# Two V groups between two score batches in a fused attention and gated MLP kernel

## The chip, the cores and the metric

One core of one Trainium2 chip. The metric is the device time of one execution in microseconds, the median of several runs. A profile of one execution gives the span from the first to the last instruction and the start of every instruction.

## The reference, cut to what matters

```python
x = A_x                                   # 1 x 2048 x 512, bf16
xn = layernorm(x)
# A: 32 heads of 16, causal window of 256 keys
qkv = xn @ wqkv                           # 512 x 1536
p = softmax(where(mask, q @ k.T * 16**-0.5, -1e9))
A = (p @ v) @ wo
# B: gate and up 512 x 1792, down 1792 x 512, no nonlinearity
B = ((xn @ w_gate) * (xn @ w_up)) @ w_down
return x + A + B
```

## The kernel before

Rows are taken in four chunks of 512. TensorE does four kinds of work. *Wide* matmuls (128 x 128 weights, 512 columns) do projections, gate, up, down and output. *Score batches* S (75 of them) use an array cut into 32 x 64 tiles and fill one PSUM tile of four banks, which one exp instruction of ScalarE empties into a P strip. *V groups* (16, one for each of the four groups `c` of eight heads in each chunk) use 64 x 32 tiles and add up two PSUM banks, which VectorE transposes. A generator issues the batches in order, and between them fills in wide work from one list, by a cost model in units of 0.216 us.

```python
self.ps_m = pool("ps_m", 4, space=PSUM)      # four banks for all wide work and V groups
self.ps_s = tc.tile_pool(name="ps_s", bufs=1, space=PSUM)   # one S tile, four banks
...
def values(self, T, c, accs=None):           # one V group
    accs = [self.ps_m.tile([128, 512], F32, tag="M", name="acc") for _ in range(2)]
    for i, (P, col, m, q, n) in enumerate(todo):          # 12 pieces (9 in chunk 0)
        for par in range(2):
            for e in range(4):
                nc.tensor.matmul(accs[par][32*e:32*e+32, q:q+n], lhsT=v, rhs=P[rows, e, col:col+n],
                                 tile_position=(64 * par, 32 * e), ...)
    for par in range(2):
        nc.vector.transpose(out=at[:, par]..., in_=accs[par][:])
...
# run(), cut: each V group follows a score batch, two batches after its own last one
for g, s in enumerate(steps):
    fill(-1, g)
    self.scores(*s)                          # S matmuls, exp, GpSimd masks
    upto = total * (g + 1) / len(steps)
    if values(g - LAG):                      # one V group, if one is due
        fill(min(spent + 4, upto), g)
        divide(g - LAG)                      # VectorE: reciprocal, multiply, transpose into OT
    for _, f in self.beside.get(g, ()):      # layernorm of the next chunk, a piece a batch
        f()
    fill(upto, g)                            # wide work
    self.mask_diag(*s)
```

The output of the chunk before, `down` and `wo`, is added to x by VectorE in `store` and leaves a `ps_m` bank there.

The softmax here doesn't subtract the row's maximum and nothing guards it: scores larger than these inputs give would overflow.

## Time and profile before

| | before |
|---|---|
| time | 266.61 us (median of 3, 266.38 to 267.07) |
| span of the profiled run | 264.5 us |
| TensorE busy | 98%, clock 1.0 |
| VectorE, ScalarE, GpSimd busy | 67%, 66%, 43% |

A busy TensorE is not the same as a streaming one. Its matmuls overlap in the records (a wide one is 0.38 us long there, and in a row one starts every 0.216 us), so what counts is the distance from one start to the next. The prediction below shows the lines and works on those distances.

### The profile page before, as it was taken

How to read it: one execution, taken by the hardware profiler on the slowest of the kernel's cores; microseconds unless marked ns; L12 is line 12 of the kernel's file. 1: busy time of each engine (PE TensorE's matmuls, PEld its weight loads, DVE VectorE, ACT ScalarE, POOL GpSimd, SP SyncE). 2: the span in 40 equal slices, each digit the busy share in tenths (PEclk: the TensorE clock that was granted, in tenths of full speed). 3: DMA queues.
4: the chain of work that ended last, by engine and by line, in shares of the span. 5: the costliest groups of instructions: out<-in, count | busy, mean ns of one | idle time of the engine just before them, and what ended most of it. 6: DMA issues, size and time to landing. Idle time of an engine off the chain costs nothing.

```text
span 264.5 us, 8898 instructions
## 1 busy us (share of the span) xinstructions
PE 258.2 (98%) x3869; PEld 120.1 (45%) x3890; DVE 178.2 (67%) x344; ACT 174.5 (66%) x139; POOL 114.9 (43%) x278
## 2 busy tenths in 40 slices
PE   8999999999999999999999999999999999999995
PEld 8444444444444444444444444444444444444453
DVE  6677898787757667667765866766752576867244
ACT  3467687788556678687765667668766576867500
POOL 6125333326674535334575443534354353344600
PEclk9999999999999999999999999999999999999999
DMA  6999911120131000002022100000200010000002
GB/s 190 379 351 342 276 21 22 24 47 4 20 90 34 22 2 1 2 2 47 2 59 66 40 2 2 0 2 4 48 2 20 25 41 2 2 0 2 4 2 79
DMA packets 19431, 15.12 MB, mean 57 GB/s; under 512 B 7360, under 2 KB 19392, under 8 KB 19392
## 3 DMA queue, kind: packets, MB, share of 16 engines
q1 hardware_dynamic: 18848, 14.26, 18.4%
q8 instruction: 30, 0.49, 0.8%
q10 hardware_dynamic: 544, 0.30, 0.4%
q14 instruction: 9, 0.07, 0.1%
HBM read 9.70 MB, written 2.10 MB: 45 GB/s over the span
## 4 chain that ended last, share of the span: by engine, by line
PE 98%; issue 1%; DVE 0%
PE up L400 19%; PE gp L389 19%; PE psd L420 16%; PE qkp L248 11%; PE S L304 10%; PE acc L358 7%; PE vp L236 5%; PE psd L426 5%; PE L L420 2%; PE wps L122 2%; PE L L426 1%; PE L L358 0%; PE xTp L207 0%; DVE y L435 0%; DVE idle L89 0%
## 5 line engine op out<-in xcount | busy, mean ns | idle before, releaser
L311 ACT ACTIVATE P<-S 128x2048 bf16<-128x2048 f32 x75 | 140.7, 1876 | 47.4 <-PE S L304 39.9
L156 POOL TENSOR_SCALAR_AFFINE_SELECT P<-P 64x256 bf16<-64x256 bf16 x224 | 98.8, 441 | 128.5 <-ACT P L311 117.6
L400 PE MATMUL up<-xnT,Wu 128*128 128x512 bf16 x224 | 60.0, 380 | 0.0
L389 PE MATMUL gp<-xnT,Wg 128*128 128x512 bf16 x224 | 58.9, 380 | 0.0
L404 DVE TENSOR_TENSOR hT<-up,gsb 128x512 bf16<-128x512 f32 x56 | 38.5, 687 | 19.5 <-PE up L400 18.0
L420 PE MATMUL psd<-Wd,hT 128*128 128x512 bf16 (+1 forms) x195 | 46.8, 368 | 1.9 <-issue 1.7
L335 DVE TENSOR_TENSOR P<-P,diag 128x512 bf16<-128x512 bf16 (+1 forms) x75 | 29.7, 397 | 10.0 <-ACT P L311 10.0
L420 PEld LDWEIGHTS <-hT 128*128 128x128 bf16 x238 | 21.2, 98 | 25.0 <-issue 2.7
L389 PEld LDWEIGHTS <-Wg 128*128 128x128 bf16 x224 | 20.7, 98 | 25.6 <-issue 1.9
L364 DVE STREAM_TRANSPOSE at<-acc 128x512 f32<-128x512 f32 x30 | 19.7, 696 | 18.6 <-PE acc L358 18.6
L400 PEld LDWEIGHTS <-Wu 128*128 128x128 bf16 x224 | 19.9, 98 | 25.0 <-issue 3.3
L304 PE MATMUL S<-Q,K 16*64 16x320 bf16 (+4 forms) x720 | 31.0, 260 | 0.1
L304 PE MATMUL S<-Q,Ko 32*64 32x320 bf16 (+4 forms) x720 | 30.9, 260 | 0.0
L227 ACT ACTIVATE gsb<-gp 128x512 bf16<-128x512 f32 x34 | 20.0, 596 | 15.5 <-PE gp L389 13.5
L248 PE MATMUL qkp<-xnT,Wqkv 128*128 128x512 bf16 x128 | 30.0, 380 | 0.0
L304 PEld LDWEIGHTS <-K 16*64 16x64 bf16 x720 | 12.1, 103 | 31.8 <-issue 31.4
L358 PE MATMUL acc<-P,VS 64*32 64x320 bf16 (+4 forms) x672 | 18.7, 254 | 0.0
L358 PE MATMUL acc<-P,V 64*32 64x320 bf16 (+4 forms) x672 | 18.5, 254 | 0.0
L248 PEld LDWEIGHTS <-Wqkv 128*128 128x128 bf16 x128 | 11.7, 98 | 14.6 <-issue 1.6
L229 DVE CAST gsb<-gp 128x512 bf16<-128x512 f32 x22 | 15.2, 691 | 3.4 <-PE gp L389 2.0
L426 PE MATMUL psd<-Wo,OT 128*128 128x512 bf16 (+1 forms) x59 | 16.2, 369 | 0.2 <-issue 0.2
L358 PEld LDWEIGHTS <-V 64*32 64x32 bf16 x720 | 14.5, 90 | 3.2 <-issue 2.6
(54 smaller groups left out, 197.0 us busy)
## 6 DMA issues: line engine op xcount, KB each, us to landing
out_dram<-y SPq DMA_DIRECT2D x15, 128.0 KB, 1.7
Wg<-in_B_w_gate_dram SPq DMA_DIRECT2D x2, 896.0 KB, 11.3
Wu<-in_B_w_up_dram SPq DMA_DIRECT2D x2, 896.0 KB, 12.5
Wd<-in_B_w_down_dram SPq DMA_DIRECT2D x1, 1792.0 KB, 17.0
Wqkv<-in_A_wqkv_dram SPq DMA_DIRECT2D x3, 512.0 KB, 6.2
x<-in_A_x_dram SPq DMA_DIRECT2D x2, 512.0 KB, 8.1
VS<-V SPq DMA_DIRECT2D x6, 144.0 KB, 2.6
x<-in_A_x_dram SPq DMA_DIRECT2D x3, 256.0 KB, 6.7
```

Of the source, the lines that this page charges most:

```text
L156: nc.gpsimd.affine_select(out=v, in_=v, pattern=pattern + [[1 if diag else -1, 64]], compare_op=ALU.is_ge if diag else ALU.is_gt, fill=0.0 ...
L227: nc.scalar.activation(out=out, in_=in_, func=ACT.Copy)
L248: nc.tensor.matmul(ps[:], lhsT=self.Wqkv[:, k, lo:lo + 128], rhs=self.xnT[T][:, :, k, :], start=(k == 0), stop=(k == 3))
L304: nc.tensor.matmul(S[64 * par:64 * par + 64, e, col:col + n], lhsT=(self.Ko if par else self.K)[U][rows, c, keys], rhs=self.Q[T][rows, c, ...
L311: nc.scalar.activation(out=P[:, :, 0:col], in_=S[:, :, 0:col], func=ACT.Exp, scale=0.25)
L335: self.nc.vector.tensor_tensor(out=v, in0=v, op=ALU.min, in1=self.diag.unsqueeze(1).unsqueeze(1).to_broadcast([128, 4, n, 64]))
L358: nc.tensor.matmul(accs[par][32 * e:32 * e + 32, q:q + n], lhsT=v, rhs=P[rows, e, col:col + n], start=(i == 0), stop=(i == len(todo) - 1), ...
L389: nc.tensor.matmul(ps[:], lhsT=self.Wg[:, k, 128 * f:128 * f + 128], rhs=self.xnT[T][:, :, k, :], start=(k == 0), stop=(k == 3))
L400: nc.tensor.matmul(ps[:], lhsT=self.Wu[:, k, 128 * f:128 * f + 128], rhs=self.xnT[T][:, :, k, :], start=(k == 0), stop=(k == 3))
L404: nc.vector.tensor_tensor(out=self.hT[T][:, f, :], in0=ps[:], in1=self.gsb[:], op=ALU.mult)
L420: nc.tensor.matmul(ps, lhsT=self.hT[T][:, f, 128 * b:128 * b + 128], rhs=self.Wd[:, f, c0:c1], start=(f == 0), stop=False)
L426: self.nc.tensor.matmul(ps, lhsT=self.OT[T][:, c, 128 * b:128 * b + 128], rhs=self.Wo[:, c, c0:c1], start=False, stop=(c == 3))
```

## The change

The intent: when two V groups stand together, with a score batch on both sides, TensorE changes its array shape four times for what took six. The places are shifted so that blocks of TensorE's instructions (in the trace of the kernel before, 30 packets of 16 KiB on an instruction queue, q8 of its DMA view) arrive in time, and score batches keep a minimum distance so that none waits for the exp before it. The diff, cut to its core:

```diff
+SCORES, VALUES, SECOND = 1.9, 6.0, 5.0
+FIRST = 3
+GAP = 9.6
+PAIRS = ((0,), (1,), (2,), (3,)), ((0, 1), (2, 3)), ((0, 1), (2, 3)), ((0, 1), (2,))
+SHIFT = {20: -2, 21: -5, 22: -8, 23: -11, 24: -14, 26: -10, 27: -7, 28: -3, 62: 3, 63: 6, 64: 8, 66: 8, 67: 6, 68: 4, 69: 2}
+MASKED, FIRST_DIVIDE, SECOND_DIVIDE = 8, 8, 24
-        self.ppool = pool("ppool", 7)
-        self.xpool = pool("xpool", 4)
-        self.ypool = pool("ypool", 4)
+        self.qpool, kpool, hpool ...            # Q, K, Ko and hT in tiles of one slice
+        self.ppool = pool("ppool", 11)
-            self.OT[T] = self.chunk2.tile(...)  # two buffers
+            self.OT[T] = self.work1.tile(...)   # one buffer
-        y = self.ypool.tile(...); add(out=y, in0=ps, in1=self.x[:, t, c0:c1])
+        y = self.x[:, t, c0:c1];  add(out=y, in0=ps, in1=y)
-    self.beside[self.first[T, 0] + (0, 2, 3, 4, 5)[i]] = fs      # layernorm of the next chunk
+    self.beside[self.first[T, 0] + (5, 6, 7, 8, 9)[i]] = fs
+    gu(T, range(FIRST))                         # three gate and up slices ahead of the downs
...
+    upto = max(total * (g + 1) / len(steps) + SHIFT.get(g, 0), spent + GAP)
+    for i, key in enumerate(keys):
+        self.values(*key)                       # one or two V groups
+    if len(keys) == 2:
+        held = s, keys                          # the next batch follows at once;
+        continue                                # masks and divides come later
```

More of the change, by code (lines that the diff above doesn't have):

```diff
@@ L23 @@
 REST = (((0, *SIX), (1, *SIX), (0, *FOUR)), ((1, *FOUR), (2, *FOUR)), ((2, *SIX), (3, *SIX), (3, *FOUR)))
-SCORES, VALUES = 1.9, 6.0
+SCORES, VALUES, SECOND = 1.9, 6.0, 5.0
[4 more added lines that the diff above has]
+MASKED, FIRST_DIVIDE, SECOND_DIVIDE = 8, 8, 24
 COPY = dict(act=2.8, dve=3.2)
@@ L43, in __init__ @@
         self.chunk2 = pool("chunk2", 2)
-        self.chunk3 = pool("chunk3", 3)
-        self.ppool = pool("ppool", 7)
+        self.qpool = pool("qpool", 5)
+        self.kpool = pool("kpool", 9)
+        self.hpool = pool("hpool", self.NF + FIRST)
+        self.ppool = pool("ppool", 11)
         self.work = pool("work", 2)
-        self.xpool = pool("xpool", 4)
         self.small = pool("small", 4)
-        self.ypool = pool("ypool", 4)
         self.work1 = pool("work1", 1)
@@ L111, in setup @@
             self.triangle(self.far[half], False)
-        self.xnT, self.Q, self.hT, self.O, self.OT = {}, {}, {}, {}, {}
+        self.xnT, self.Q, self.hT, self.OT = {}, {}, {}, {}
         self.K, self.Ko, self.V, self.VS = {}, {}, {}, {}
@@ L124, in new_chunk @@
     def new_chunk(self, T):
-        self.Q[T] = self.chunk2.tile([128, 4, 512], BF16, tag="Q", name=f"Q{T}")
-        self.K[T] = self.chunk3.tile([128, 4, 512], BF16, tag="K", name=f"K{T}")
-        self.Ko[T] = self.chunk3.tile([128, 4, 512], BF16, tag="Ko", name=f"Ko{T}")
         self.V[T], self.VS[T] = self.stock[T % 3]
@@ L186, in norm_apply @@
         mv, j, rs = self.stats.pop(t)
-        xn = self.xpool.tile([128, 512], BF16, tag="xn", name="xn")
+        xn = self.work.tile([128, 512], BF16, tag="xn", name="xn")
         nc.vector.tensor_scalar(out=xn[:], in0=self.x[:, t, :], scalar1=mv[:, j, 0:1],
@@ L210, in bank @@
     def bank(self, ks, name):
+        self.open = 3 not in ks
         if 0 in ks:
@@ L251, in proj_qk @@
             return
-        self.copy((self.K if is_k else self.Q)[T][:, c, :], ps[:], engine)
         if is_k:
-            nc.vector.tensor_scalar(out=self.Ko[T][:, c, :], in0=self.K[T][:, c, :],
+            self.K[T, c] = self.kpool.tile([128, 512], BF16, tag="K", name="K")
+            self.Ko[T, c] = self.kpool.tile([128, 512], BF16, tag="Ko", name="Ko")
+        else:
+            self.Q[T, c] = self.qpool.tile([128, 512], BF16, tag="Q", name="Q")
+        self.copy((self.K if is_k else self.Q)[T, c][:], ps[:], engine)
+        if is_k:
+            nc.vector.tensor_scalar(out=self.Ko[T, c][:], in0=self.K[T, c][:],
                                     scalar1=self.odd[:, 0:1], scalar2=None, op0=ALU.mult)
@@ L304, in scores @@
                     nc.tensor.matmul(S[64 * par:64 * par + 64, e, col:col + n],
-                                     lhsT=(self.Ko if par else self.K)[U][rows, c, keys],
-                                     rhs=self.Q[T][rows, c, q:q + n],
+                                     lhsT=(self.Ko if par else self.K)[U, c][rows, keys],
+                                     rhs=self.Q[T, c][rows, q:q + n],
                                      start=True, stop=True, tile_position=(32 * e, 64 * par),
@@ L360, in values @@
                                      tile_position=(64 * par, 32 * e), skip_group_check=True)
-        at = self.work1.tile([128, 2, 16, 32], F32, tag="at", name="at")
+        at = self.work.tile([128, 2, 16, 32], F32, tag="at", name="at")
         for par in range(2):
@@ L374, in divide @@
         if c == 0:
-            self.OT[T] = self.chunk2.tile([128, 4, 512], BF16, tag="OT", name=f"OT{T}")
-        on = self.work.tile([128, 16, 2, 16], BF16, tag="on", name="on")
+            self.OT[T] = self.work1.tile([128, 4, 512], BF16, tag="OT", name=f"OT{T}")
+        on = self.work1.tile([128, 16, 2, 16], BF16, tag="on", name="on")
         nc.vector.tensor_tensor(out=on.rearrange("p b r d -> p r b d"), in0=at[:, :, :, 0:16],
@@ L384, in gate @@
         nc = self.nc
-        if f == 0 and 0 in ks:
-            self.hT[T] = self.const.tile([128, self.NF, 512], BF16, tag="hT", name=f"hT{T}")
         ps = self.bank(ks, "gp")
@@ L403, in up @@
             return
-        nc.vector.tensor_tensor(out=self.hT[T][:, f, :], in0=ps[:], in1=self.gsb[:], op=ALU.mult)
+        self.hT[T, f] = self.hpool.tile([128, 512], BF16, tag="hT", name="hT")
+        nc.vector.tensor_tensor(out=self.hT[T, f][:], in0=ps[:], in1=self.gsb[:], op=ALU.mult)
         self.book("dve", COPY["dve"])
@@ L409, in down @@
         nc = self.nc
+        self.open = True
         if lo == 0 and part == 0:
@@ L419, in down @@
             ps, c0, c1 = self.sums[b][part]
-            nc.tensor.matmul(ps, lhsT=self.hT[T][:, f, 128 * b:128 * b + 128],
+            nc.tensor.matmul(ps, lhsT=self.hT[T, f][:, 128 * b:128 * b + 128],
                              rhs=self.Wd[:, f, c0:c1], start=(f == 0), stop=False)
@@ L431, in store @@
         nc = self.nc
+        self.open = False
         t = 4 * T + b
         ps, c0, c1 = self.sums[b][part]
-        y = self.ypool.tile([128, 512], BF16, tag="y", name="y")[:, 0:c1 - c0]
-        nc.vector.tensor_tensor(out=y, in0=ps, in1=self.x[:, t, c0:c1], op=ALU.add)
+        y = self.x[:, t, c0:c1]
+        nc.vector.tensor_tensor(out=y, in0=ps, in1=y, op=ALU.add)
         self.book("dve", COPY["dve"])
@@ L463, in project, with gu @@
                 qk(T, c, self.first[T, c])
-        def gu(T, between):
-            for f in range(NF):
+        def gu(T, fs, between={}):
+            for f in fs:
                 for ks in halves:
@@ L498, in fillers @@
                     for i, fs in norms(T + 1, 0, 1).items():
-                        self.beside[self.first[T, 0] + (0, 2, 3, 4, 5)[i]] = fs
-                down(T - 1, 0)
-                wo(T - 1, 0, (0, 1))
+                        self.beside[self.first[T, 0] + (5, 6, 7, 8, 9)[i]] = fs
+                gu(T, range(FIRST))
                 for b in range(4):
-                    if b < 3:
-                        down(T - 1, b + 1, range(0, NF - 2, 2))
-                    wo(T - 1, b, (2, 3))
+                    down(T - 1, b)
+                    wo(T - 1, b, range(4))
                     add(0, lambda T=T, b=b: self.store(T - 1, b))
-                    if b < 3:
-                        down(T - 1, b + 1, range(NF - 2, NF, 2))
-                        wo(T - 1, b + 1, (0, 1))
-            gu(T, norms(1, 1, 3) if T == 0 else {})
+                gu(T, range(FIRST, NF))
+            else:
+                gu(T, range(NF), norms(1, 1, 3))
             if T + 1 < NCH:
@@ L523, in run @@
         self.setup()
-        NCH, LAG = self.NCH, 2
+        NCH = self.NCH
         RESERVE = 31.5
@@ L533, in run @@
                 steps.append((T, pieces))
-        due = {g: key for key, g in self.last.items()}
+        due = {}
+        for T in range(NCH):
+            for cs in PAIRS[T]:
+                due[self.last[T, cs[-1]] + 3 - len(cs)] = [(T, c) for c in cs]
         self.beside = {}
         work = self.fillers()
-        total = sum(w[0] for w in work) - RESERVE + SCORES * len(steps) + VALUES * (len(due) - 1)
+        total = sum(w[0] for w in work) - RESERVE + SCORES * len(steps)
+        total += sum(VALUES + SECOND * (len(keys) - 1) for keys in due.values())
         spent, n = 0, 0
         self.free = dict(act=0, dve=0)
-        valued, ready = -1, -1
+        valued, ready, pending = -1, -1, []
         def fill(upto, group):
@@ L554, in fill, with divide @@
                 n += 1
-        def values(g):
-            nonlocal spent
-            if g not in due:
-                return False
-            spent += VALUES
-            self.now = spent
-            self.values(*due[g])
-            return True
-        def divide(g):
+                while pending and spent >= pending[0][0]:
+                    pending.pop(0)[1]()
+        def divide(key):
             nonlocal ready
-            self.divide(*due[g])
-            ready = g
+            self.divide(*key)
+            ready = self.last[key]
+        held = None
         for g, s in enumerate(steps):
-            fill(-1, g)
-            valued = ready
+            keys = due.get(g, [])
+            if held is None:
+                valued = ready
+                fill(-1, g + len(keys) // 2)
+                while len(keys) == 2 and self.open:
+                    fill(spent + work[n][0] / 2, g)
             spent += SCORES
@@ L575, in run @@
             self.scores(*s)
-            upto = total * (g + 1) / len(steps)
+            upto = max(total * (g + 1) / len(steps) + SHIFT.get(g, 0), spent + GAP)
             if g in (1, 2):
                 self.new_values()
-            if values(g - LAG):
+            for i, key in enumerate(keys):
+                spent += SECOND if i else VALUES
+                self.now = spent
+                self.values(*key)
+            if len(keys) == 2:
+                held = s, keys
+                continue
+            if held is not None:
+                pending += [(spent + MASKED, lambda s=held[0]: self.mask_diag(*s)),
+                            (spent + FIRST_DIVIDE, lambda key=held[1][0]: divide(key)),
+                            (spent + SECOND_DIVIDE, lambda key=held[1][1]: divide(key))]
+                held = None
+            for key in keys:
                 fill(min(spent + 4, upto), g)
-                divide(g - LAG)
+                divide(key)
             for _, f in self.beside.get(g, ()):
@@ L593, in run @@
         fill(spent + 10, -1)
-        self.values(*due[len(steps) - 1], self.late)
+        self.values(T, 3, self.late)
         spent += VALUES
-        divide(len(steps) - 1)
+        divide((T, 3))
         valued = ready
```

## The prediction

> **What bounds the kernel now.** I read the page's busy table first, then the chain that ended last, the waits of TensorE, and last the timeline of one trip of TensorE from wide matmuls through a score batch and a V group and back.
>
> ```profile
> PE 258.2 (98%) x3869; PEld 120.1 (45%) x3890; DVE 178.2 (67%) x344; ACT 174.5 (66%) x139; POOL 114.9 (43%) x278
> PE   8999999999999999999999999999999999999995
> PEclk9999999999999999999999999999999999999999
> PE 98%; issue 1%; DVE 0%
> ```
>
> TensorE (PE) is busy in every slice at the full granted clock, VectorE and ScalarE are a third idle, and the chain that sets the end is 98% TensorE. Only less work or fewer bubbles on TensorE can shorten the program. Does TensorE wait for anybody? The waits view of that engine has four rows in all:
>
> ```profile
> PE psd L420 <- issue: 1.7, 11, 0.2
> PE wps L122 <- DVE idle L89: 1.1, 1, 1.1
> PE psd L426 <- issue: 0.2, 1, 0.2
> PE L L420 <- issue: 0.2, 1, 0.2
> ```
>
> The 1.1 us is the start. The others are 13 gaps of 0.2 us, each the length of one wide matmul. The busy table has 3869 matmuls beside 3890 weight loads, so 21 records are missing, and I read these gaps as missing records, not as idle time. So no wait for another engine is there to be removed. What remains is time that is busy on paper but streams nothing, and only start-to-start distances show it. The timeline of TensorE, lines left out inside the V group:
>
> ```profile
> 110.14 1.03 PE L400 MATMUL up<-xnT,Wu 128*128 128x512 bf16 x4
> 111.10 0.28 PE L304 MATMUL S<-Q,K 16*64 16x192 bf16 x4
> 111.11 0.28 PE L304 MATMUL S<-Q,Ko 32*64 32x192 bf16 x4
> 111.20 0.30 PE L304 MATMUL S<-Q,K 16*64 16x320 bf16 x4
> 111.22 0.30 PE L304 MATMUL S<-Q,Ko 32*64 32x320 bf16 x4
> 111.45 0.26 PE L358 MATMUL acc<-P,V 64*32 64x192 bf16 x4
> ...
> 112.50 0.29 PE L358 MATMUL acc<-P,VS 64*32 64x256 bf16 x4
> 112.73 0.60 PE L389 MATMUL gp<-xnT,Wg 128*128 128x512 bf16 x2
> ```
>
> Inside a row of wide matmuls one starts every 0.216 us (four of them, 0.38 us long each, span 1.03). The last of the four starts at 110.79 and the score batch at 111.10: 0.309 us, so 0.093 us more than streaming. The last score matmul starts at about 111.23 and streams 320 columns, 0.133 us at 2.4 columns per ns; V starts at 111.45, 0.224 later: 0.091 lost. V's last matmul, 256 columns (0.107 us), starts at about 112.53; the wide ones resume 0.202 us later: 0.095 lost. Over all 75 score batches and 16 V groups the medians of these distances are the same: wide to S 0.309, S to V 0.224, V to wide 0.202, S to wide 0.227 (0.094 lost). After a return the first two wide matmuls are 0.227 apart and not 0.216: another 0.011. So **each change of array shape costs about 0.093 us** wherever it occurs. The 75 batches and 16 groups make 167 changes, some 15.5 us of the 264.5.
>
> [...]its instruction queue of TensorE moves 0.49 MB in 30 packets, 16 KiB each, and in the packet records they take 0.91 to 1.92 us, median 1.08. [...]No run yet shows a stall from it: the twelve V groups of the later chunks, 192 instructions each, all have 1.077 to 1.080 us between first and last start.
>
> **The change part by part.** Before, each V group follows a score batch of its own: wide, S, V, wide, three changes of shape. After, for chunks 1 and 2 (two pairs each) and chunk 3 (one pair), two V groups stand between two score batches: wide, S, V, V, S, wide. Chunk 0 and the last two heads groups of chunk 3 stay single. Five pairs.
>
> Two trips before: 2 x (0.093 + 0.091 + 0.095 + 0.011) = 0.580 us of loss.
> One double trip after: wide to S 0.093, S to V 0.091, V to V about 0.010, V to S about 0.094, S to wide 0.094, first pair of wide ones 0.011: 0.393 us.
> V to V keeps the shape. A V group has 12 pieces; 1.079 us to its last start, less 0.96 us for the 2304 columns before the last piece, leaves 0.12 for 11 boundaries, so 0.010 each. V to S doesn't occur before; I take the price of the other changes.
> **Saving: 0.187 us a pair, 0.93 us for five.** All of it is on the path, since TensorE waits for nobody and is the chain.
>
> The rest of the diff moves no TensorE time by itself. The count of matmuls is the same. Q, K, Ko and hT become tiles of one slice each, P gets 11 buffers in place of 7, the result is written over x in place of a y buffer: these allow the new order (the first head group's five strips live longer: five and five batches and the one just issued make 11) and add no instruction. Three gate and up slices now come before the down projections of the chunk before, and norm work moves by a few batches; same work. The new minimum distance between score batches (9.6 units of 0.216 us, 2.07 us of wide work) prevents a wait that the kernel before doesn't have: all 75 batches start 0.309 us after the last wide matmul (the longer ones by a missing record), and the closest pair of batches is 2.71 us apart.
>
> 266.61 - 0.93 = 265.68, say **265.7 us**.
>
> **The rivals.**
> *Instruction fetch takes it back.* A pair issues 2 x (32 to 48) + 2 x 192, so 448 to 480 instructions, in about 3.2 us (0.36 + 1.19 + 1.28 + 0.36). 256 instructions then last 1.6 us in the V groups, against 1.08 us for the transfer of a block[...]; today a block lasts 3.5 us at the least (shortest interval between packets). Against it: the change picks its five places for this, by shifts of single batches. For it: the margin is under 0.5 us, and it was set by trial. If half the pairs lose 0.5 us, the time is about 267; if all five lose 1 us, 270.
> *The second score batch waits for exp.* There is one S buffer. From S to the second S there are 0.35 + 1.19 + 1.28 = 2.82 us. An exp starts 0.56 us after its batch's first matmul (median of 75) and takes 1.88, done at 2.44; today's closest batch comes 0.24 us after the exp's end without delay. Slack 0.14 to 0.38 us. A PSUM copy of 0.60 us just ahead of the exp would turn it into 0.1 to 0.3 us of waiting: at worst 1.5 us over five pairs, 267.
> *PSUM banks.* Two V groups hold all four buffers of the shared pool. The transposes of a group are done 0.72 and 1.32 us after its last matmul. The first group's are done within V's second 1.19 us and the score batch; the second group's are needed only after two more banks of wide work, 0.36 + 1.73 us later. Slack of about 0.8 us, unless VectorE has other work in front; the masks and divides are deferred for that. Likely nothing, at worst 0.5 us.
> *More is gained than the switches.* There is no wait to remove, so I see no way below about 265.
>
> **Range and chances.** The middle is 265.7. The repeats of the kernel before spread by 0.7 us (266.38 to 267.07), so the median of three is good to some 0.3. One or two pairs with a stall of half a microsecond give 266.2 to 266.7. I take 265.1 to 266.6 for 8 in 10. Faster by over 2% would need 261.3, six times the saving: 1%. Slower by over 2% needs 271.9, a stall of over 1 us in each pair: 2%. Within 2%: 97%.
>
> **What would show each step.** Right: five places in the timeline with S, V, V, S; 157 changes of shape in place of 167; [...]V to S losing some 0.09; a shorter span with the same matmuls; and still no wait of TensorE for ScalarE, VectorE or anything else. Wrong: V starts inside a pair further apart than 0.01 us beyond streaming (fetch), a wait of S for exp or of wide matmuls for the transposes, or a last stretch, after the last V group, that is longer than the 11.5 us of before because the pacing leaves too little wide work there.

The rate of 2.4 columns per ns is in the trace of the kernel before (512 columns every 0.216 us). The 256 instructions of a block are near what the same trace gives as a mean, 257: from the start of the first packet to that of the thirtieth 3732 weight loads start, each with its matmul, so 7464 instructions over 29 packets. The chances and sizes of the stalls (half a microsecond, one microsecond) were estimates.

## The result

| | before | changed |
|---|---|---|
| time, 6 runs each | 266.39 us (266.23 to 267.07) | 265.39 us (265.04 to 265.44) |
| span of the profiled run | 264.5 us | 263.7 us |
| first score batch to start of last V group (trace) | 239.48 us | 238.70 us |

The ratio is 0.9956 (95% interval 0.9943 to 0.9969). Ratios here are the mean time of one kernel's runs over that of the other's of the same rounds, so not quite the ratio of the medians. The result is 1.0 us faster, within 2%, inside the predicted range and near the predicted 265.7.

The third row of the table is the measure that I use from here on: from the first matmul of the first score batch to the first matmul of the last V group. Both kernels do the same TensorE work in that stretch (3650 weight loads, each with its matmul), and it leaves out the start, which varies by some tenths of a microsecond between profiles, and the end.

The changed kernel's page, its busy table, TensorE's row of slices and the chain that ended last:

```profile
PE 259.6 (98%) x3890; PEld 120.3 (46%) x3890; DVE 174.2 (66%) x341; ACT 175.9 (67%) x142; POOL 117.3 (44%) x278
PE   7999999999999999999999999999999999999995
PE 97%; DVE 1%; DMA 1%; issue 0%
```

This time all 3890 matmuls are recorded, and the 13 gaps called "issue" of the kernel before are gone, so they were missing records indeed. TensorE is the bound as before. Its waits:

```profile
PE wps L127 <- DVE idle L94: 1.1, 1, 1.1
PE xTp L209 <- DVE xn L190: 0.3, 1, 0.3
```

Both are at the start. By this view nobody holds TensorE up later. The timeline of TensorE at pair 2 (wide, S, V, V, S, wide; the lines inside the V groups left out) shows the new trip:

```profile
123.31 0.81 PE L251 MATMUL qkp<-xnT,Wqkv 128*128 128x512 bf16 x3
124.05 0.28 PE L312 MATMUL S<-Q,K 16*64 16x192 bf16 x4
...
124.41 0.26 PE L366 MATMUL acc<-P,V 64*32 64x192 bf16 x4
...
125.46 0.29 PE L366 MATMUL acc<-P,VS 64*32 64x256 bf16 x4
125.54 0.27 PE L366 MATMUL acc<-P,V 64*32 64x192 bf16 x4
...
126.58 0.29 PE L366 MATMUL acc<-P,VS 64*32 64x256 bf16 x4
126.81 0.28 PE L312 MATMUL S<-Q,K 16*64 16x192 bf16 x4
...
126.93 0.30 PE L312 MATMUL S<-Q,Ko 32*64 32x320 bf16 x4
127.16 1.04 PE L251 MATMUL qkp<-xnT,Wqkv 128*128 128x512 bf16 x4
```

The first V group's last matmul starts at 125.49 (the fourth of the row at 125.46) and the second group begins 0.051 us later, although that last matmul, of 256 columns, streams for 0.107. (The rate is in the traces: V to wide takes 0.149 us after a last piece of 128 columns and 0.202 after one of 256, so 2.4 columns per ns.) At a change of shape the same distance is 0.199 to 0.202. So V to V doesn't just avoid the price of a change of shape, it overlaps, by 0.056 us.

**Counting one pair cleanly.** Before, two trips take, in distances from start to start, 2 x (0.130 within S + 0.224 + 1.079 within V + 0.202) plus 2 x (0.093 + 0.011) at the wide work: 3.478 us. Pair 2 takes 0.130 + 0.224 + 2.200 + 0.199 + 0.130 + 0.226, plus 0.104: 3.213 us. The saving is **0.265 us a pair**, 1.325 us for five. The trace shows only 239.48 - 238.70 = 0.78 us. Where is the other half microsecond? The five pairs don't look alike. Their V runs, from the first to the last start, in the first profile:

| pair | 1 | 2 | 3 | 4 | 5 |
|---|---|---|---|---|---|
| V run, ns | 2357 | 2200 | 2401 | 2199 | 2369 |

Pairs 1, 3 and 5 lose 0.157, 0.201 and 0.169 us, together 0.53, and 1.325 - 0.53 = 0.80. That closes the account. The waits view doesn't show these losses: the recorded end of a matmul lies after its streaming (0.29 us after the start at 256 columns, which stream for 0.107), so a short wait disappears under it.

**Pair 1.** The timeline of all engines there:

```profile
89.25 0.57 POOL L182 TENSOR_TENSOR rs<-ve,mhalf 128x1 f32<-128x1 f32 x1
...
89.85 0.48 DVE L190 TENSOR_SCALAR xn<-x,mv,rs 128x512 bf16<-128x512 bf16 x1 [1.27 <-POOL rs L182]
...
90.25 0.67 DVE L444 TENSOR_TENSOR x<-psd,x 128x512 bf16<-128x512 f32 x1
...
90.76 0.29 PE L366 MATMUL acc<-P,VS 64*32 64x256 bf16 x4
...
90.98 0.26 PE L366 MATMUL acc<-P,V 64*32 64x192 bf16 x4
```

The second V group's first piece starts 0.256 us after the piece before it, and not 0.109 as in pair 2. Its weight load waits on VectorE's semaphore alone and starts 0.06 us after VectorE has finished (90.92) the output add that empties a bank. (The matmul itself waits on GpSimd's semaphore; GpSimd's masks had ended at 90.67.) That add stood in VectorE's queue behind a layernorm instruction, xn, which had waited 1.27 us for GpSimd's rs. Pair 3 has the same pattern: its second V matmul row starts at 155.73, just after a VectorE copy that ended at 155.67 and had itself come after an xn that waited 1.27 us for rs.

**Pair 5.** TensorE's timeline:

```profile
222.71 0.27 PE L366 MATMUL acc<-P,V 64*32 64x192 bf16 x4
222.76 0.49 PE L366 MATMUL acc<-P,VS 64*32 64x320 bf16 x4
222.95 0.32 PE L366 MATMUL acc<-P,V 64*32 64x320 bf16 x4
```

Here a gap of 0.165 us from start to start lies in the middle of a group, before a matmul that waits on no semaphore. The trace's record of the last block packet before it in TensorE's instruction queue has it from 220.59 to 221.55.

### The profile page after: what moved, and what is told of

Same layout as the page of the kernel before. It is cut to its first block, busy times and chain, and to the rows that moved or that the text cites. A ratio compares the mean times of both kernels' runs of the same rounds, so it can differ in the third digit from the quotient of the medians.

```text
span 263.7 us, 8896 instructions
## 1 busy us (share of the span) xinstructions
PE 259.6 (98%) x3890; PEld 120.3 (46%) x3890; DVE 174.2 (66%) x341; ACT 175.9 (67%) x142; POOL 117.3 (44%) x278
## 4 chain that ended last, share of the span: by engine, by line
PE 97%; DVE 1%; DMA 1%; issue 0%
PE gp L395 19%; PE up L406 19%; PE psd L428 17%; PE qkp L251 11%; PE S L312 10%; PE acc L366 7%; PE vp L239 5%; PE psd L434 5%; PE L L428 2%; DMA x<-in_A_x_dram 1%; DVE st L169 1%; PE L L434 1%; PE L L366 0%; PE xTp L209 0%; DVE xn L190 0%; DVE mv L170 0%
## 5 line engine op out<-in xcount | busy, mean ns | idle before, releaser
L158 POOL TENSOR_SCALAR_AFFINE_SELECT P<-P 64x256 bf16<-64x256 bf16 x224 | 101.3, 452 | 126.0 <-ACT P L319 111.6
L395 PE MATMUL gp<-xnT,Wg 128*128 128x512 bf16 x224 | 60.2, 380 | 0.0
L406 PE MATMUL up<-xnT,Wu 128*128 128x512 bf16 x224 | 58.8, 380 | 0.0
L428 PE MATMUL psd<-Wd,hT 128*128 128x512 bf16 (+1 forms) x210 | 48.0, 369 | 0.0
L343 DVE TENSOR_TENSOR P<-P,diag 128x512 bf16<-128x512 bf16 (+1 forms) x75 | 29.1, 388 | 9.5 <-ACT P L319 9.5
L406 PEld LDWEIGHTS <-Wu 128*128 128x128 bf16 x224 | 20.6, 98 | 25.6 <-issue 2.3
L230 ACT ACTIVATE gsb<-gp 128x512 bf16<-128x512 f32 x40 | 23.5, 596 | 7.5 <-PE gp L395 6.7
L444 DVE TENSOR_TENSOR x<-psd,x 128x512 bf16<-128x512 f32 (+1 forms) x15 | 9.7, 653 | 16.4 <-PE psd L434 16.4
L251 PEld LDWEIGHTS <-Wqkv 128*128 128x128 bf16 x128 | 11.7, 98 | 14.5 <-issue 1.6
L366 PE MATMUL acc<-P,VS 64*32 64x320 bf16 (+4 forms) x672 | 18.0, 253 | 0.0
L239 PE MATMUL vp<-Wqkv,xnT 128*128 128x512 bf16 x64 | 15.3, 380 | 0.0
```

The lines of the kernel that those rows point to most:

```text
L158: nc.gpsimd.affine_select(out=v, in_=v, pattern=pattern + [[1 if diag else -1, 64]], compare_op=ALU.is_ge if diag else ALU.is_gt, fill=0.0 ...
L230: nc.scalar.activation(out=out, in_=in_, func=ACT.Copy)
L239: nc.tensor.matmul(ps[:], lhsT=self.xnT[T][:, b, k, :], rhs=self.Wqkv[:, k, 1024:1536], start=(k == 0), stop=(k == 3))
L251: nc.tensor.matmul(ps[:], lhsT=self.Wqkv[:, k, lo:lo + 128], rhs=self.xnT[T][:, :, k, :], start=(k == 0), stop=(k == 3))
L343: self.nc.vector.tensor_tensor(out=v, in0=v, op=ALU.min, in1=self.diag.unsqueeze(1).unsqueeze(1).to_broadcast([128, 4, n, 64]))
L366: nc.tensor.matmul(accs[par][32 * e:32 * e + 32, q:q + n], lhsT=v, rhs=P[rows, e, col:col + n], start=(i == 0), stop=(i == len(todo) - 1), ...
```

## The experiments

My theory at this point: ten changes of shape are saved, 0.265 us a pair; at pairs 1 and 3 a PSUM bank comes late from VectorE, because of the layernorm's new place; at pair 5 a block of instructions comes late. The rivals: parts of the rest of the change give the gain; all three losses are fetches; or pair 5 waits for another engine. Each edit is to the changed kernel unless it says otherwise. The V runs of the pairs, in ns, collected:

| run | pair 1 | 2 | 3 | 4 | 5 | first S to start of last V, us |
|---|---|---|---|---|---|---|
| before (no pairs) | | | | | | 239.48 |
| changed | 2357 | 2200 | 2401 | 2199 | 2369 | 238.70 |
| e2 norms earlier | 2199 | 2198 | 2197 | 2199 | 2199 | 238.15 |
| e3 8 places earlier | 2619 | 2199 | 2596 | 2872 | 2199 | 239.65 |
| e4 8 places later | 2619 | 2198 | 2592 | 2199 | 2199 | 239.12 |
| e6 no shifts | 2546 | 2200 | 2397 | 2199 | 2881 | 241.20 |
| e7 norms, shift 12 | 2199 | 2198 | 2199 | 2199 | 2198 | 238.16 |
| e11 e7 again | 2200 | 2200 | 2199 | 2199 | 2201 | 238.17 |
| e12 changed again | 2366 | 2198 | 2401 | 2199 | 2305 | 238.63 |

### e1: the rest of the change alone

```diff
-PAIRS = ((0,), (1,), (2,), (3,)), ((0, 1), (2, 3)), ((0, 1), (2, 3)), ((0, 1), (2,))
-SHIFT = {20: -2, ...}
+PAIRS = (((0,), (1,), (2,), (3,)),) * 3 + (((0,), (1,), (2,)),)
+SHIFT = {}
```

> The changed kernel with all V groups single and no shifts; every other part of the change stays (smaller tiles, result over x, three gate and up slices first, later norms, minimum distance). Theory (the gain is the ten fewer changes of array shape and nothing else): back to the time of the kernel before, 266.4 us within 0.4, ratio to before 0.998 to 1.002, with 167 changes of shape in the trace. Rival (the rest of the change gives part of the gain): 265.9 or less.

Measured: 282.08 us, ratio 1.0597 (1.0566 to 1.0629). The expectation missed by 16 us. Lines of its waits, all engines:

```profile
DVE OT L388 <- PE psd L434: 20.2, 3, 7.3
...
PE up L406 <- DVE x L444: 6.5, 2, 4.7
...
PE gp L395 <- DVE x L444: 4.3, 2, 4.0
```

VectorE stood before three OT transposes for 20.2 us in all, and TensorE then stood 10.8 us for VectorE. Beside its two longest gaps the granted clock was 0.5 for 6.8 us each (wide matmuls up to 0.38 us apart). The three are the first of chunks 1, 2 and 3. With one OT buffer such a transpose has to wait until the last output projection of the chunk before has read OT. With pairs it comes later (in chunk 1 at 95.7 us of the changed kernel's trace, against 83.9 in the kernel before, which has two buffers), and by then the buffer is free. So "adds no instruction" was not "costs nothing": this buffer fits the paired order alone.

### e5 and e9: the rest again, with two OT buffers, then with the old norm places

```diff
 # both with e1's edit, and:
-            self.OT[T] = self.work1.tile(...)
+            self.OT[T] = self.chunk2.tile(...)
-        self.ppool = pool("ppool", 11)
+        self.ppool = pool("ppool", 10)
 # e9 in addition
-        self.beside[self.first[T, 0] + (5, 6, 7, 8, 9)[i]] = fs
+        self.beside[self.first[T, 0] + (0, 2, 3, 4, 5)[i]] = fs
```

> As e1_singles (which took 282.1 us), but with two buffers of OT as the kernel before has, and 10 buffers of P in place of 11 to make room. Theory (e1 lost its 16 us because a chunk's first OT transpose has to wait until the last output projection of the chunk before has read the only OT buffer, 6.4, 6.4 and 7.3 us on VectorE; all else in the change costs nothing): 266.0 to 266.7 us, ratio 0.998 to 1.002, and no idle VectorE of over 1 us before an OT transpose. Rival (other parts, such as three gate and up slices first or the y written over x, cost or save by themselves): off by more than that.

e5 measured 267.6 us (267.47 to 267.66), ratio 1.0042 (1.0028 to 1.0055). The OT waits are gone, but the time is 1.1 us over the kernel before. Its waits have one row after the start that the kernel before doesn't:

```profile
PE up L406 <- DVE x L444: 0.9, 2, 0.5
```

Twice, at 93.36 and 158.43, an up matmul starts 0.84 and 0.85 us after the one before it in place of 0.216: 1.26 us, and the stretch from the first S to the last V is 240.74, 1.26 longer than before. Just ahead VectorE has the same sequence as at pair 1 of the changed kernel: xn after 1.27 and 0.77 us of waiting for rs, then the output add that frees the bank.

> As e5_singles_ot2 (single V groups, two OT buffers, 267.6 us), with the norm work back at the batches where the kernel before has it. Theory (e5's extra 1.1 us is its two waits of 0.63 us of a gate or up matmul for a bank that VectorE empties late, because the changed kernel issues the norms later, among the output adds): those two waits vanish and the time is that of the kernel before, 266.1 to 266.7 us, ratio 0.998 to 1.002. Rival (three gate and up slices first or y over x cost by themselves): 267 us or more.

e9 measured 266.25 us (266.07 to 266.43), ratio 0.9994 (0.998 to 1.0008), and 239.48 us from first S to last V, exactly that of the kernel before. So the later norms cost, and what is left of the change (the first three gate and up slices, the smaller tiles, the result over x and the rest) costs and saves nothing in sum. The gain in this stretch comes from the pairs.

### e2: the norms two batches earlier

```diff
-        self.beside[self.first[T, 0] + (5, 6, 7, 8, 9)[i]] = fs
+        self.beside[self.first[T, 0] + (3, 4, 5, 6, 7)[i]] = fs
```

> The norm work of the next chunk is issued two batches earlier, so that VectorE is not held by it at pairs 1 and 3. In the changed kernel the V runs of the five pairs last 2357, 2200, 2401, 2199 and 2369 ns from first to last start. Theory (pairs 1 and 3 wait for a PSUM bank that VectorE empties late, behind a norm instruction that waits for GpSimd): pairs 1 and 3 fall to about 2200 ns, pair 5 stays at about 2370, and the time falls by some 0.35 us to about 265.0. Rival (these are instruction fetches): the positions in the instruction stream are unchanged, so 2357 and 2401 stay.

Measured: 265.32 us, but from 264.74 to 266.17, ratio 0.9954 (0.9932 to 0.9976); too wide to tell from the changed kernel's by time. The profiled run lost 1.1 us at its start to a late load of Wqkv. The traces are clear: pairs 1 and 3 fell to 2199 and 2197 with the order of TensorE's instructions unchanged. Pair 5 fell too, which I had not expected; its block packet started 1.14 us ahead of the first V matmul and not 0.74. So an unchanged order alone doesn't rule out fetches, as I had meant it to. What does, for pairs 1 and 3, is that their late weight loads wait on VectorE's semaphore and stand at the places 201 and 241 of 256 in the changed kernel, while the fetch gaps below all stand at 191.

### e3 and e4: the whole program moved against the blocks

```diff
-        self.keep_busy(40)
+        self.keep_busy(36)     # e4: 44
```

> Four idle warm-up matmuls fewer at the start (36 in place of 40), so that all later instructions stand 8 places earlier against the 256-instruction blocks, with the same order and the same waits. Theory (pair 5 waits for a block of instructions[...]): pair 5 gets 4 wide matmuls (0.86 us) less of lead, so its V run grows from 2369 to about 3000 to 3200 ns, and pair 4 now stands where pair 5 stood and grows from 2199 to about 2370; the time rises by some 0.8 to 1.2 us to about 266.4. Rival (pair 5 waits for another engine): all five V runs within 30 ns of what they were.

The shorter lead, four matmuls of 0.216 us, was an estimate; what starts a packet no trace shows.

e3 measured 266.45 us, ratio 1.0001 (0.9986 to 1.0016). Pair 4, now at pair 5's old place, went from 2199 to 2872. Its waits have the row

```profile
PE acc L366 <- issue: 0.4, 1, 0.4
```

with no engine named. But pair 5 itself, expected to get worse, went to 2199; its packet started at -1.13. A place alone doesn't decide, the packet's start does. So the time, 266.45 against an expected 266.4, was hit by luck: other losses than the expected ones made it up. Pairs 1 and 3 grew to 2619 and 2596 although their wait is for VectorE.

> Four warm-up matmuls more (44), so that all later instructions stand 8 places later against the blocks. Theory (fetch at pair 5): pair 5 now stands where pair 4 stood and falls from 2369 to about 2200 ns; pairs 1 and 3 keep 2357 and 2401, since they wait for VectorE; the time falls by 0.15 us to about 265.2, less up to 0.1 if the longer warm-up delays the start. Rival (another engine): pair 5 stays at 2369.

e4 measured 265.84 us, ratio 0.9986 (0.9971 to 1.0001), against an expected 265.2. Pair 5 fell to 2199 as the theory said and pair 4 stayed. Pairs 1 and 3 were expected to stay, but, as in e3, they were 0.26 and 0.19 us longer than in the first profile, long enough for the waits view to show part of them and to name VectorE's output add and its copy of gsb:

```profile
PE acc L366 <- DVE x L444: 0.2, 1, 0.2
PE acc L366 <- DVE gsb L232: 0.2, 1, 0.2
```

At pair 1 of e4 GpSimd's rs ends 0.37 us after the first V matmul, in the first profile 0.11, and xn and the add follow: the whole shift of 0.26. A third loss of 0.14 us is a block wait outside the pairs (below). The three, less the 0.17 that pair 5 gained, make up the 0.42 us by which the stretch is longer than the changed kernel's. Why GpSimd runs in one of two phases is open; e3 and e4 have the later, e12 and e6's pair 3 the earlier.

### e6: without the shifts

```diff
-SHIFT = {20: -2, ...}
+SHIFT = {}
```

> The changed kernel with the shifts taken out. The V run of pair 5 then begins 16 places earlier against the blocks of 256 and that of pair 1 24 places later; pairs 2 to 4 stand where they stood. Theory (a pair waits for a block when the packet of its block starts later than 0.91 us before the first V matmul; so far 0.17 us of wait at a start of -0.74 and 0.67 us at -0.25): pair 5 shows the wait that this rule gives for its packet, and it is longer than the 0.17 us of the changed kernel, so V run about 2600 to 3400 ns and the time 0.3 to 1.2 us longer, 265.7 to 266.6. Rival (the places don't matter): pair 5 at 2200 to 2370 ns and 265.4 us.

Measured: 267.88 us (267.59 to 268.09), ratio 1.0052 (1.0038 to 1.0066): slower than the kernel before, and 1.3 us over what I had allowed. Pair 5 shows 2881, within the range, 0.68 us of wait; the rule said 0.75. What I had missed is pair 1, whose second score batch stops in its middle:

```profile
95.18 0.30 PE L312 MATMUL S<-Q,Ko 32*64 32x320 bf16 x3
96.98 0.32 PE L312 MATMUL S<-Q,Ko 32*64 32x320 bf16 x1 [1.50 <-issue]
```

This wait of 1.79 us, 0.51 more at pair 5 and 0.19 more at pair 1, where a bank came late, make up the 2.50 us by which the stretch grew. So both shifted places matter, and without the shifts the pairs are a loss.

### The block waits together

Six gaps within pairs, over all runs, are on a matmul that waits on no semaphore. I numbered TensorE's instructions in program order and looked up the packet of the block queue that came last before the gap's end:

| run, pair | place in 256 of the instruction after the gap | packet start before first V, us | packet took, us | packet end to resumption, us | gap, us |
|---|---|---|---|---|---|
| changed, pair 5 | 191 | -0.74 | 0.96 | 1.40 | 0.165 |
| e12, pair 5 | 191 | -0.82 | 0.93 | 1.43 | 0.103 |
| e3, pair 4 | 191 | -0.25 | 1.00 | 1.37 | 0.674 |
| e6, pair 5 | 191 | -0.16 | 0.95 | 1.49 | 0.693 |
| e6, pair 1 | 191 | +2.01 | 1.24 | 1.41 | 1.792 |
| e8, chunk 0 | 191 | +0.74 | 1.15 | 1.46 | 1.789 |

All six stop at the same place modulo 256, as they would at the border of a block of 256 instructions (in the changed kernel's trace too 3732 weight loads, each with its matmul, start between the starts of the first and the thirtieth packet, 257 instructions a packet), and all resume 1.37 to 1.49 us after their packet has ended. Counted from the start, the packet of each gap is also the one of the block that begins there. A seventh gap of this kind stands outside the pairs, in e4 at 129.06: a gate matmul starts 0.355 us after the one before it in place of 0.216, at place 191, 1.27 us after its packet of 1.35 us had ended. At the other borders of this count, 29 in each of the 14 traces, no block was entered sooner after its packet's end than 1.37 us. At all other pairs of chunks 1 to 3 the last packet ahead of the first V matmul started 1.1 us or more before it, and none shows a gap of this kind over 0.02 us. That pair 5 waits for instructions I call shown. Which event starts a packet is not: at one and the same place the start was -0.74, -0.82, -1.14 and -1.18 us.

### e7 and e11: both repairs; e12: the changed kernel beside it

```diff
-        self.beside[self.first[T, 0] + (5, 6, 7, 8, 9)[i]] = fs
+        self.beside[self.first[T, 0] + (3, 4, 5, 6, 7)[i]] = fs
-SHIFT = {..., 62: 3, 63: 6, 64: 8, 66: 8, ...}
+SHIFT = {..., 62: 3, 63: 6, 64: 12, 66: 8, ...}
```

> Norms two batches earlier as in e2, and the shift before pair 5 at 12 in place of 8, which puts it 8 places later, where pair 4 never waited. Theory: all five V runs at 2200 ns, no wait of TensorE after the start; the change's full saving of 0.265 us in each of five pairs, 1.33 us, so about 265.0 us, 0.4 to 0.5 us under the changed kernel and ratio about 0.995 to before. If a DMA of the start is late by a microsecond in the profiled run, as in e2, that shows before 10 us and is no part of it.

Measured: 264.86 us (264.83 to 264.99), ratio 0.994 (0.9928 to 0.9953). The waits of TensorE, all of them:

```profile
PE psd L428 <- issue: 1.1, 7, 0.2
PE wps L127 <- DVE idle L94: 1.1, 1, 1.1
PE vp L239 <- issue: 0.2, 1, 0.2
PE L L428 <- issue: 0.2, 1, 0.2
```

Gaps of 0.2 us are missing records again. All five V runs are 2198 or 2199, and the stretch from first S to last V is 238.16, that is 1.32 us under the kernel before, beside the 1.325 worked out from pair 2 alone.

> The kernel of e7 again, beside the changed kernel on one chip: 264.8 to 265.0 us, all V runs of the pairs at 2200 ns.

> The changed kernel unaltered, in the same rounds as e11. Theory (it loses some 0.5 us, varying with the phase of GpSimd and of the instruction packets, at pairs 1, 3 and 5): 265.2 to 265.6 us, 0.3 to 0.7 us over e11, and a wider spread than e11's; the V runs of pairs 1, 3 and 5 over 2200 ns by amounts that differ from those of its first profile, those of pairs 2 and 4 at 2200.

On one chip: e11 264.79 us (264.76 to 265.13), ratio 0.9942 (0.9929 to 0.9954); e12 265.24 us (265.16 to 265.71), ratio 0.9961 (0.9948 to 0.9973). The repaired kernel is 0.45 us faster than the changed one in the medians, and its trace 0.46 us shorter (238.63 against 238.17). This version beats both kernels.

### e8 and e10: pairs in chunk 0 too

```diff
 # e8, on e2's kernel
-PAIRS = ((0,), (1,), (2,), (3,)), ...
+PAIRS = ((0, 1), (2, 3)), ...
 # e10, on e7's kernel
+PAIRS = ((0, 1), (2,), (3,)), ...
```

> As e2 with pairs in chunk 0 as well, seven in all. Theory (a pair is good only where its two V groups outlast the exp): in chunk 0 a V group has 9 pieces and 0.86 to 0.96 us, so from S to second S there would be 0.35 + 0.81 + 0.96, about 2.1 us, while the exp ends 2.44 us after S; each of the two pairs in chunk 0 waits 0.4 to 0.6 us before its second S and saves 0.27, so the time is 0.2 to 0.8 us above e2's level of 265.0, and the distance from last V to S there is 0.6 to 0.8 us in place of 0.2. Rival (switches alone count): 0.5 us below e2, 264.5 us.

e8 measured 266.36 us, ratio 0.9996 (0.9981 to 1.0012). Its waits have

```profile
PE acc L366 <- issue: 1.5, 1, 1.5
```

at the second pair of chunk 0, the block wait of the table. The first pair waited for the exp, by 0.22 us (V to S 0.419 and not 0.199, on ScalarE's semaphore), so the mechanism was right and its size half of what I expected. The time is 1.4 us over the 265.0 named there, above the range, and the larger part of that is the block wait.

> As e7 with one pair in chunk 0, heads 0 and 1, which in e8 stood clear of a late block but waited 0.22 us for the exp before its second score batch. Theory (the exp wait eats the saving of the two switches, 0.265 us): 264.7 to 265.0 us, no gain over e7's 264.86 beyond 0.15 us, with a V to S distance of about 0.4 us at that pair. Rival (switches alone count): 264.6 us and V to S of 0.2 us.

e10, without the pair that fell on a late block, measured 264.85 us (264.77 to 265.23), ratio 0.9946 (0.993 to 0.9961), no gain over e11's 264.79 of the same rounds. Its waits have this row, where e11's have none of the kind:

```profile
PE S L312 <- ACT P L319: 0.2, 1, 0.2
```

From first S to the start of the last V it is 238.21 us, 0.04 longer than e11. This pair saves less than the later ones, some 0.17 us: V to V is 0.074 and not 0.051, and its second group lasts 0.814 us, 0.057 more than alone in e11, where the second groups of the later pairs last 0.011 less than alone. The exp wait of 0.22 takes more than that.

## Why the prediction was right or wrong

**Right, with two sizes off that nearly cancel.** 265.7 was predicted, 265.4 came. That the number is so near is partly luck: the saving was 0.39 us larger than its middle estimate, and losses of 0.53 us, which the middle left to the rivals, took it back. Of its signs the five places, 157 changes of shape in place of 167 and a last stretch of 11.5 us as before came true. That TensorE waits for nobody did not.

- *TensorE is the only bound, and the 13 gaps are missing records.* Right. The changed kernel's full record shows none.
- *A change of shape costs about 0.093 us.* Right: wide to S 0.309, S to V 0.224 and S to wide 0.227 are the same after. V to S, taken as 0.094, measured 0.199 - 0.107 = 0.092.
- *V to V costs about 0.010.* This term was mis-sized. It measured 0.051 - 0.107 = -0.056, and the second group takes 0.011 less in itself. I had taken the price of a border inside a group from the last start, though a piece's eight matmuls start over some 0.056 us while the next piece's already follow. The saving is 0.265 us a pair, not 0.187; e7 shows five times that, 1.32 us.
- *The rest of the diff moves no TensorE time by itself.* Wrong. The norm work's later place costs: 1.26 us in e5's single order, 0.36 us at pairs 1 and 3. The single OT buffer costs 14.5 us without pairs (e1 against e5); with them no wait for it shows. The other parts cost nothing in sum (e9).
- *Rival, PSUM banks: likely nothing, at worst 0.5 us.* It happened, 0.157 + 0.201 us in the first profile, and in e3, over the worst case named, 0.419 + 0.396. My reason for "nothing" looked only at the time from the transposes to the wide work after the pair, and not at the banks that the pair itself has to get.
- *Rival, instruction fetch.* It happened at one pair, 0.17 us, less than the half microsecond a pair that I had named; e6 shows that it is the largest danger, a gap of 1.79 us at one place. My margin of some 0.5 us set the 1.6 us that 256 instructions last in a pair against the 1.08 us that a packet takes in the median. In the table a block could be used only 2.36 to 2.65 us after its packet had started, so there was no margin: it takes a packet that starts early.
- *Rival, exp.* It doesn't happen in the later chunks (V to S 0.199 to 0.200 us at all five pairs), and does in chunk 0, 0.22 us in e8 and in e10, where V groups are shorter (9 pieces and not 12).
- *The sum.* 1.325 - 0.53 = 0.80 us worked out, 0.78 in the trace, 1.0 us in the medians; 0.93 was predicted. The 0.2 us between trace and medians lie outside the first to the last instruction: the device time is 1.67 to 1.78 us longer than this span in every run of the changed kernel and its variants, and 1.91 us on average in the repeats of the kernel before. It is no gain of the pairs, since e9, without pairs, has it too (1.70). Its cause is open.

## What to carry to other kernels

Joining two groups of one array shape saved two changes of shape of 0.093 us here and won 0.056 us of overlap too, so measure a join inside an existing group, start to start, before pricing it. When the engine that bounds all is waiting for nobody, look at whether the new order makes it ask for buffers in bursts: here two groups at once wanted four banks and twice the instructions, and whatever else stands in the other engines' queues then, such as a norm that waits 1.27 us for GpSimd, becomes visible. Waits of 0.16 to 0.20 us under overlapping matmuls showed in no waits view; compare equal groups with each other.
